# The first loads of a fused attention and feed-forward kernel: another order on the two queues, no touch load, and other fillers on TensorE

## The chip, the cores and the metric

The kernel runs on one core of one Trainium2 chip. The metric is the device time in microseconds (us) of one execution.

## The reference, cut to what matters

```python
x = A_x                                        # 2048 x 640, bf16
g = sigmoid((x * gate_w).sum(-1))
qkv = x @ wqkv                                 # 640 -> 3 * 640
pq, pk = phi(q), phi(k)                        # phi(t) = where(t > 0, t + 1, exp(t)) + 1e-6
a = linear_attention(pq, pk, v) @ wo
b = (gelu(x @ w_gate) * (x @ w_up)) @ w_down   # the larger part
return g * a + (1 - g) * b
```

The change touches only the first 9 us or so: the loading of x and of the K and Q columns of `wqkv`, and the first two of the sixteen 128-row tiles of x, which TensorE transposes itself. All other tiles are transposed by DMA while they are loaded.

## The kernel before

The kernel is a list of operations for each engine. A helper, `P.op`, works out the waits from what each operation reads and writes. `"sp"` is SyncE's DMA queue, `"act"` is ScalarE's. Chunk k of `wk` holds rows 128k to 128k+127 of the K columns; a load of one chunk, or of one tile of x, is 160 KB.

```python
P.op("act", lambda e: e.dma_start(touch[0:16, 0:4], A_wqkv[0:128:8, 640:644]),
     writes=[P.res("touch")], dma=new_dma_key())          # the "touch": 0.1 KB, never read
load_x(0)
load_wk(0)
load_x(1, "act")
load_wk(1)
load_wk(3)
# ... ScalarE's first activation, which loads its table
load_wk(2, "act")
load_wk(4, "act")
# ... gate_w on "act"
for k in range(KC):                                       # KC = 5
    load_wq(k, ("sp", "act")[k % 2])
# ... then on "sp": the transposing loads of x tiles 2 to 15, the first one after wk chunk 4 has landed
```

On TensorE, `warm(count, n)` issues fillers: matmuls of constants with n columns, whose result nobody reads. `T(i, ks, bank)` transposes chunks `ks` of x tile i into a bank of PSUM (the memory that TensorE writes to), and VectorE copies them from there into `xT`. `KM(i, [k])` is the pair of matmuls (512 and 128 columns) of tile i with wk chunk k. `QM` is the same for Q.

```python
def T(i, ks, tb):
    # ... transposes into psb[:, tb, ...]
    P.op("pe", fn, reads=[r_xn[i], r_ident], writes=[bank[tb]])
    P.op("dve", lambda e: e.tensor_copy(xT[:, ks[0]:ks[-1] + 1, i * 128:(i + 1) * 128], ...),
         reads=[bank[tb]], writes=[...])

warm(5, 512)
warm(1, 128)
T(0, [0], 7)
T(0, [1, 2, 3, 4], 6)
warm(6, 128)
KM(0, [0])
T(1, [0], 7)
T(1, [1, 2, 3, 4], 6)
warm(3, 128)
KM(1, [0])
for k in (1, 2, 3):
    KM(0, [k])
    KM(1, [k])
gate_col()
# ... KM(0, [4]), KM(1, [4]), then QM for both tiles, all five chunks
```

## Time and profile before

| | before |
|---|---|
| median of 3 executions | 274.09 us (273.87 to 274.1) |
| span of the profiled execution | 272.2 us (its device time: 273.55 us) |
| x tile 0 landed / wk chunk 0 landed | 3.0 / 4.24 us |
| first K matmul / first Q matmul | 4.38 / 7.67 us |

The page of the kernel before gives the span, and then each engine's busy time with its share of the span. PE is TensorE, PEld its weight loads, DVE VectorE, ACT ScalarE and POOL GpSimd; below, SPq and ACTq are the queues of SyncE and ScalarE, and PEq is TensorE's sequencer.

```profile
span 272.2 us, 3426 instructions
...
PE 267.9 (98%) x1343; PEld 128.1 (47%) x1369; DVE 141.8 (52%) x251; ACT 75.9 (28%) x132; POOL 30.0 (11%) x28
```

TensorE is busy for 98% of the span, so only its head can give anything. Below is TensorE's timeline of the kernel before. The columns are start, duration (both in us), engine, line, operation with its operands, and count; at the end stands the idle time before it, with what ended that. Consecutive instructions of one kind are merged.

```profile
0.82 2.40 PE L417 MATMUL ps<-const-bfloat16-1.0 128*128 128x512 bf16 x6 [0.82 <-PEq L911]
3.02 0.74 PE L431 MATMUL ps<-pool 128*128 128x128 bf16 x5
3.55 0.62 PE L417 MATMUL ps<-const-bfloat16-1.0 128*128 128x128 bf16 x6
4.38 0.38 PE L451 MATMUL ps<-pool 128*128 128x512 bf16 x1 [0.21 <-DMA pool<-in_A_wqkv_dram]
...
4.64 0.44 PE L431 MATMUL ps<-pool 128*128 128x128 bf16 x5
...
5.18 0.39 PE L451 MATMUL ps<-pool 128*128 128x512 bf16 x1
...
6.01 0.38 PE L451 MATMUL ps<-pool 128*128 128x512 bf16 x1
...
7.67 0.38 PE L466 MATMUL ps<-pool 128*128 128x512 bf16 x1
7.88 0.22 PE L467 MATMUL ps<-pool 128*128 128x129 bf16 x1
```

L417 is the fillers, L431 the transposes, L451 and L452 a K pair, L466 and L467 a Q pair. The first six fillers (five of 512 columns, one of 128) run from 0.82 to 3.02 us. That is 0.43 us for each wide one, twice what a wide matmul takes later: the K pairs that follow each other at 0.27 us contain one wide matmul (0.22 us) and one narrow one. TensorE's clock is still low there. The six narrow fillers at 3.55 us are the place where it rises.

Next come two of the waits of TensorE and of its weight loads in the first 12 us. The columns are who waited for what, us in total, times, and the longest.

```profile
PE ps L451 <- DMA pool<-in_A_wqkv_dram: 0.2, 1, 0.2
```

```profile
PEld ps L451 <- DVE pool L435: 0.4, 1, 0.4
```

The first K pair waited 0.2 us for wk chunk 0; the weight load of tile 1's first K pair waited for VectorE's copy. The next lines are from the chain of work that ended last, in order of time (start, us, what):

```profile
1.26 2.98 DMA pool<-in_A_wqkv_dram
...
4.38 0.38 PE ps L451
...
10.32 0.71 ACT pool L476
...
16.89 9.15 PE ps L536 x49
```

The chain starts with the load of wk chunk 0 (issued at 1.26 us). It goes through the K and Q matmuls, then through ScalarE and VectorE until 16.9 us, and from there through TensorE to the end. So whatever moves the first Q matmul should move the end by as much. Last, the first two DMA issues (size, us from issue to landing):

```profile
pool<-in_A_x_dram SPq DMA_DIRECT2D x1, 160.0 KB, 2.2
pool<-in_A_wqkv_dram ACTq DMA_DIRECT2D x1, 0.1 KB, 2.0
```

x tile 0, issued at 0.79 us, landed 2.2 us later. The touch of 0.1 KB took 2.0 us, so the whole of x tile 0 costs only 0.2 us more than a load of almost nothing.

### The profile page before, as it was taken

The numbers are of one execution on the slowest core, as the hardware profiler recorded it, in microseconds if no ns is written. First come the engines' busy times: TensorE is split into PE (matmuls) and PEld (weight loads), VectorE is DVE, ScalarE is ACT, GpSimd is POOL, SyncE is SP. The second block draws the span as 40 slices with busy tenths as digits, with TensorE's granted clock in tenths as the row PEclk, the third lists the DMA queues.
The fourth block names the chain that finished last, engine by engine and source line by source line (L and its number), as shares of the span: only waits on it lengthen the run. The fifth ranks groups of instructions, "written<-read, shape, count | busy, mean of one in ns | idle before, by whom it ended". The sixth has DMA issues, their size and how long they took to land.

```text
span 272.2 us, 3426 instructions
## 1 busy us (share of the span) xinstructions
PE 267.9 (98%) x1343; PEld 128.1 (47%) x1369; DVE 141.8 (52%) x251; ACT 75.9 (28%) x132; POOL 30.0 (11%) x28
## 2 busy tenths in 40 slices
PE   8999999999999999999999999999999999999997
PEld 4555555544445444444444444444444444444444
DVE  2689898997333335999999999634110000000200
ACT  2555555210422453332222232224011122121021
POOL 5000000003140002242332421000000000000000
PEclk9999999999999999999999999999999999999999
DMA  6776999500300011612221221272031110110211
GB/s 219 176 114 124 349 402 384 119 2 19 61 16 2 23 50 51 200 28 48 27 48 30 43 50 25 60 229 96 5 79 37 41 39 19 39 41 19 58 58 41
DMA packets 42208, 23.61 MB, mean 87 GB/s; under 512 B 31567, under 2 KB 40783, under 8 KB 42063
## 3 DMA queue, kind: packets, MB, share of 16 engines
q1 hardware_dynamic: 41429, 22.56, 30.5%
q10 hardware_dynamic: 762, 0.82, 0.8%
q8 instruction: 11, 0.18, 0.3%
q14 instruction: 6, 0.05, 0.1%
HBM read 13.83 MB, written 2.63 MB: 60 GB/s over the span
## 4 chain that ended last, share of the span: by engine, by line
PE 95%; DVE 2%; DMA 1%; issue 1%; ACT 1%; SPq 0%; DVEq 0%; ACTq 0%
PE ps L697 41%; PE ps L861 23%; PE ps L536 12%; PE ps L593 6%; PE ps L840 4%; PE ps L808 2%; PE ps L675 2%; PE ps L596 2%; DMA pool<-in_A_wqkv_dram 1%; PE ps L451 1%; PE ps L821 1%; PE ps L466 1%; DVE pool L490 1%; PE ps L718 1%; DVE pool L555 1%
## 5 line engine op out<-in xcount | busy, mean ns | idle before, releaser
L697 PE MATMUL ps<-pool 128*128 128x512 bf16 x510 | 113.0, 379 | 0.5
L697 PEld LDWEIGHTS ps<-pool 128*128 128x128 bf16 x520 | 50.4, 98 | 60.1
L861 PE MATMUL ps<-pool 128*128 128x512 bf16 (+2 forms) x300 | 62.4, 367 | 0.3
L703 ACT ACTIVATE pool<-ps 128x512 f32<-128x512 f32 x52 | 31.0, 597 | 73.1 <-PE ps L697 73.1
L705 DVE TENSOR_TENSOR pool<-ps,pool 128x512 bf16<-128x512 f32 x52 | 34.6, 689 | 31.7 <-PE ps L697 30.4
L861 PEld LDWEIGHTS ps<-pool 128*128 128x128 bf16 x306 | 29.1, 98 | 33.5 <-issue 0.4
L536 PE MATMUL ps<-pool 128*128 128x512 bf16 (+1 forms) x206 | 37.9, 344 | 0.2
L844 DVE TENSOR_TENSOR pool<-ps,pool 128x512 bf16<-128x512 f32 x4 | 2.8, 692 | 61.5 <-PE ps L840 61.5
L751 POOL TENSOR_TENSOR pool<-pool 128x640 f32<-128x640 bf16 x16 | 22.5, 1406 | 72.8 <-DVE pool L753 65.9
L868 ACT ACTIVATE pool<-ps,pool 128x512 bf16<-128x512 f32 (+1 forms) x16 | 10.9, 680 | 68.6 <-PE ps L861 68.6
L536 PEld LDWEIGHTS ps<-pool 128*128 128x128 bf16 x210 | 20.5, 98 | 17.5
L555 DVE SCALAR_TENSOR_TENSOR pool<-ps,pool 128x128 bf16<-128x128 f32 (+2 forms) x42 | 25.3, 603 | 2.4
L546 ACT ACTIVATE pool<-ps 128x640 bf16<-128x640 f32 x28 | 19.7, 703 | 18.1 <-DVE pool L555 10.6
L593 PE MATMUL ps<-pool 128*128 128x512 bf16 x76 | 19.2, 380 | 0.1
L761 DVE TENSOR_TENSOR pool<-pool 128x640 bf16<-128x640 bf16 x16 | 13.2, 825 | 0.6
L759 DVE TENSOR_SCALAR pool<-pool 128x32 f32<-128x32 f32 x16 | 12.8, 803 | 0.6
L753 DVE TENSOR_REDUCE pool<-pool 128x32 f32<-128x640 f32 x16 | 12.9, 809 | 0.0
L641 DVE TENSOR_TENSOR pool<-pool 128x640 f32<-128x640 f32 x14 | 11.6, 826 | 0.5
L840 PE MATMUL ps<-pool 128*128 128x512 bf16 x51 | 11.5, 380 | 0.1
L643 POOL PARTITION_ALL_REDUCE pool<-pool x1 | 4.0, 3971 | 60.7 <-DVE pool L641 60.7
L593 PEld LDWEIGHTS ps<-pool 128*128 128x128 bf16 x78 | 6.9, 98 | 7.2
L552 DVE TENSOR_SCALAR pool<-pool 128x640 bf16<-128x640 bf16 x28 | 9.1, 327 | 1.8 <-ACT pool L546 0.4
(70 smaller groups left out, 105.0 us busy)
## 6 DMA issues: line engine op xcount, KB each, us to landing
out_dram<-pool SPq DMA_DIRECT2D x19, 128.0 KB, 1.7
pool<-in_B_w_gate_dram SPq DMA_DIRECT2D x1, 2080.0 KB, 14.2
pool<-in_B_w_up_dram SPq DMA_DIRECT2D x1, 2080.0 KB, 18.8
pool<-in_A_x_dram SPq DMA_DIRECT2D x1, 1280.0 KB, 8.7
pool<-in_B_w_down_dram SPq DMA_DIRECT2D x1, 1120.0 KB, 6.1
pool<-omg_row SPq DMA_DIRECT2D x1, 1024.0 KB, 4.8
pool<-in_A_wqkv_dram SPq DMA_DIRECT2D x6, 160.0 KB, 4.4
pool<-in_A_x_dram SPq DMA_DIRECT2D x1, 960.0 KB, 5.8
```

The source lines that it names most:

```text
L536: last = e.matmul(ps[:, b + p, 0:c1 - c0], xT[:, k, i * 128:(i + 1) * 128], wkq[:, k, c0:c1], start=(k == 0), stop=(k == KC - 1))
L546: P.op("act", lambda e: e.activation(e_buf[m], ps_flat[:, o:o + 640], ACT.Exp), reads=banks, writes=[r_e[m]])
L555: P.op("dve", lambda e, c0=c0, c1=c1: e.scalar_tensor_tensor(dst[:, c0:c1], ps_flat[:, o + c0:o + c1], 1.0 + EPS, e_buf[m][:, c0:c1], ALU. ...
L593: last = e.matmul(ps[:, b, :], pk[i][:, c * 128:(c + 1) * 128], x_aug[:, i, 0:512], start=(i == 0), stop=(i == NT - 1))
L697: last = e.matmul(ps[:, b, :], w[:, k, fc * 128:(fc + 1) * 128], xT[:, k, j * 512:(j + 1) * 512], start=(k == 0), stop=(k == KC - 1))
L703: P.op("act", lambda e: e.activation(ge[n], ps[:, gb, :], ACT.Gelu_apprx_tanh), reads=[bank[gb]], writes=[r_ge[n]])
L705: P.op("dve", lambda e: e.tensor_tensor(hT[fc][:, j * 512:(j + 1) * 512], ps[:, ub, :], ge[n], ALU.mult), reads=[bank[ub], r_ge[n]], write ...
L751: P.op("pool", lambda e: e.tensor_tensor(tmp[n], pq[i], z_b, ALU.mult), reads=[r_pq[i], r_zb], writes=[r_tmp[n]])
L753: P.op("dve", lambda e: e.tensor_reduce(den[n], tmp[n].rearrange("p (h d) -> p h d", h=32), AX.X, ALU.add), reads=[r_tmp[n]], writes=[r_de ...
L761: P.op("dve", lambda e: e.tensor_tensor(pq[i].rearrange("p (h d) -> p h d", h=32), pq[i].rearrange("p (h d) -> p h d", h=32), den[n].unsqu ...
L840: last = e.matmul(ps[:, b, :], wd[:, fc, 512:640], hT[fc][:, j * 512:(j + 1) * 512], start=False, stop=(fc == NFC - 2), skip_group_check=True)
L861: last = e.matmul(ps[:, pb, 0:c1 - c0], lhs, rhs, start=False, stop=(q == len(rows) - 1), skip_group_check=True)
```

## The change

The intent is to have x tile 0 and wk chunk 0 arrive together at the heads of both queues, then tile 1 and chunk 1. The touch load goes. TensorE gets two more wide fillers, so that it stays busy until x tile 0, now sharing the bandwidth, lands. Tile 0's second K pair is drawn forward, and three fillers stand in front of the pairs of chunk 2.

```diff
--- before.py
+++ after.py
@@ -352,22 +352,20 @@
                 dma_in(wq[:, k, 0:640], A_wqkv[k * 128:(k + 1) * 128, 0:640], [r_wq[k]], eng=eng)
 
 
-            P.op("act", lambda e: e.dma_start(touch[0:16, 0:4], A_wqkv[0:128:8, 640:644]),
-                 writes=[P.res("touch")], dma=new_dma_key())
             load_x(0)
-            load_wk(0)
-            load_x(1, "act")
-            load_wk(1)
-            load_wk(3)
+            load_wk(0, "act")
+            load_x(1)
+            load_wk(1, "act")
+            load_wk(2)
+            load_wk(4)
 
             zero = nc.const_aps.tensor(0.0, (128, 1), F32)
             P.op("act", lambda e: e.activation(eg[:, 0:1], zero, ACT.Exp), writes=[r_eg[0]])
-            load_wk(2, "act")
-            load_wk(4, "act")
+            load_wk(3, "act")
             P.op("dve", lambda e: e.memset(gw_sb, 0.0), writes=[r_gw])
             dma_in(gw_sb[0:5, :], gate_w.rearrange("(k p) -> k p", p=128), [r_gw], eng="act")
             for k in range(KC):
-                load_wq(k, ("sp", "act")[k % 2])
+                load_wq(k, ("act", "sp")[k % 2])
 
             def load_xT(i, after=()):
                 P.op("sp", lambda e: e.dma_start_transpose(xT[:, :, i * 128:(i + 1) * 128],
@@ -500,17 +498,19 @@
 
 
             ALLK = list(range(KC))
-            warm(5, 512)
-            warm(1, 128)
+            warm(7, 512)
+            warm(2, 128)
             T(0, [0], 7)
             T(0, [1, 2, 3, 4], 6)
-            warm(6, 128)
+            warm(3, 128)
             KM(0, [0])
             T(1, [0], 7)
             T(1, [1, 2, 3, 4], 6)
+            KM(0, [1])
+            KM(1, [0])
+            KM(1, [1])
             warm(3, 128)
-            KM(1, [0])
-            for k in (1, 2, 3):
+            for k in (2, 3):
                 KM(0, [k])
                 KM(1, [k])
             gate_col()
```

## The prediction

> **What bounds it now.** TensorE is busy in 98% of the 272.2 us span (engine table), so only the head can give anything. TensorE's timeline: fillers from 0.82 us; transposes of x tile 0 at 3.02; first K matmul at 4.38, after a 0.21 us wait for wk chunk 0; transposes of x tile 1 at 4.64; then K pairs every 0.27 us; first Q matmul at 7.67. From there the chain of waits runs through the Q matmuls, ScalarE and VectorE (10.3 to 16.9 us), then TensorE to the end: a shift of the first Q matmul should pass on one for one.
>
> **Loads before** (landing, DMA view): x0 3.0, wk0 4.24, x1 4.4, wk1 5.4, wk2 5.6, wk3 6.2, wk4 6.5, wq0 7.4 us: 160 KB at 3.0, then 320 KB per 1.0 to 1.3 us. The Trainium skill ("DMA: Bandwidth & Descriptors", "Issuing engines are not separate DMA queues") says that issuing from two engines only saves issue time; the trace agrees: pairs share about 300 GB/s.
>
> **After, costed.**
> - x0 shares the head with wk0 in place of a 0.1 KB touch. Estimate: both land near 3.5 (half a pair after the old x0). wk0 gains 0.7 us, x0 loses 0.5.
> - Seven fillers of 512 columns. Until about 3.7 us the trace shows them 0.43 us apart (half rate; 128-column ones then go from 107 to 56 ns). The Trainium skill ("TensorE: Matmul & The Clock Gate", "What's actually happening") has TensorE start at half rate until a busy window of about 3.4 us has passed; here that ends near 3.7. So the fillers end near 3.85 and themselves hold x0's transposes, 0.8 us later than before, though at full rate.
> - From a transpose group's start to its first K matmul: 0.54 us (tile 1: 4.64, copy 4.90, matmul 5.18). So KM(0,0) starts near 4.40, against 4.38: the wait for wk0 goes, VectorE's copy behind a late transpose stands in its place.
> - x1 and wk1 land near 4.8 (4.5 to 5.0): x1 later than its 4.4, wk1 earlier than 5.4. T(1) starts near 4.8 instead of 4.64.
> - KM(1,1) needs tile 1's second copy (copies last 0.65 us from 0.26 after the transposes' start): about 5.8 (before 5.74). Three fillers (0.17 us) now follow: KM(0,2) near 6.2 (before 6.01). wk2, wk3 (5.9) and wk4 (6.6) are in time; six pairs and the gate column take 1.65 us: first Q matmul at 7.75 to 7.95, against 7.67.
> - wq chunks land within 0.2 us of before, with 0.3 us or more of slack: hidden.
>
> All of the change lies on the critical path, but its parts cancel: -0.2 us (wk0), +0.2 to +0.4 (late transposes, x1 later, fillers before k=2). After the first Q matmul the instructions are the same.
>
> **Predicted: 274.2 us, 8 in 10 between 273.7 and 274.7. Faster by over 2%: 0.005; within 2%: 0.985; slower: 0.01.**
>
> **What would show the steps.** x0 and wk0 landing near 3.5; T(0) near 3.85 right behind a filler; no wait for wk0; T(1) starting on x1's landing; KM(1,1) released by VectorE's copy; first Q matmul 0.1 to 0.3 us later; the 10.3 to 16.9 us stretch shifted by as much.
>
> **What would make it wrong.** Two queues fill faster at the start (gain up to 0.2 us); x0 landing past 3.9; the clock rising at another moment, which moves the fillers' end by up to 0.4 us; a wq chunk or the first transposing load of x becoming late.

## More of the kernel before

The trace's record of the granted clock has its first entry, full clock, at 3.77 us. **The profile's own row of granted clocks does not show this.** Here are two windows of the kernel before; the columns are the window, its length, the busy time and count of each engine, then the granted clock, the DMA share and GB/s:

```profile
0.00:2.00 2.00, 1.18 (x3) 0.43 (x4) 0.11 (x1) 0.29 (x1) 1.12 (x7) 1.00 0.07 19
2.00:4.00 2.00, 2.00 (x15) 1.27 (x13) 0.43 (x2) 1.20 (x2) 1.86 (x3) 1.00 0.89 253
```

Both say 1.00, although the first two microseconds ran at half rate: nothing is recorded before the rise. At the head of a kernel the clock has to be read from the durations.

## The result, and the profile after

| | before | after |
|---|---|---|
| median | 274.10 us (4 executions, 273.87 to 274.29) | 274.33 us (4 executions, 273.76 to 274.76) |
| ratio after / before | | 1.0008, 95% interval 0.9986 to 1.0029 |
| the same in two more sessions | | 1.0006 (0.9993 to 1.0019) and 1.0017 (1.0005 to 1.0029) |

A ratio is the mean time of one kernel's fast runs over that of the other's fast runs of the same rounds, so it is not quite the ratio of the medians. The three sessions put the change at 0.2 to 0.5 us slower, though only the third interval excludes no change at all: "the same" at the 2% level, and close to the predicted 274.2 us.

The execution that was profiled after the change was the slowest of its four (274.76 us), whereas the one profiled before (273.55 us) was faster than the four other executions of it in this comparison. The two traces therefore exaggerate the difference.

TensorE's timeline after (L415 fillers, L429 transposes, L449 and L450 K pairs, L464 and L465 Q pairs):

```profile
0.83 3.36 PE L415 MATMUL ps<-const-bfloat16-1.0 128*128 128x512 bf16 x9 [0.83 <-PEq L911]
4.03 0.56 PE L429 MATMUL ps<-pool 128*128 128x128 bf16 x5
...
4.64 0.39 PE L449 MATMUL ps<-pool 128*128 128x512 bf16 x1
...
4.92 0.59 PE L429 MATMUL ps<-pool 128*128 128x128 bf16 x5
...
6.03 0.39 PE L449 MATMUL ps<-pool 128*128 128x512 bf16 x1
...
6.31 0.34 PE L415 MATMUL ps<-const-bfloat16-1.0 128*128 128x128 bf16 x3
7.30 0.39 PE L449 MATMUL ps<-pool 128*128 128x512 bf16 x1 [0.66 <-DMA pool<-in_A_wqkv_dram]
...
8.97 0.38 PE L464 MATMUL ps<-pool 128*128 128x512 bf16 x1
9.19 0.22 PE L465 MATMUL ps<-pool 128*128 128x129 bf16 x1
```

The transposes of tile 0 start at 4.03 us, 1.0 us later than before. The first K pair at 4.64 us is only 0.26 us later, and it no longer waits for a load. The pairs of chunk 2 come at 7.30 us instead of 6.01, after a wait of 0.66 us; the first Q matmul comes at 8.97 us instead of 7.67. The waits view (0 to 12 us) says the same, and shows a wait for VectorE, which copies tile 1:

```profile
PE ps L449 <- DMA pool<-in_A_wqkv_dram: 0.7, 1, 0.7
```

```profile
PEld ps L449 <- DVE pool L433: 0.3, 1, 0.3
```

The DMA issues after: first the two at the heads of the queues, then wk chunk 2 (issued at 1.72 us).

```profile
pool<-in_A_wqkv_dram ACTq DMA_DIRECT2D x1, 160.0 KB, 3.0
pool<-in_A_x_dram SPq DMA_DIRECT2D x1, 160.0 KB, 3.2
```

```profile
pool<-in_A_wqkv_dram SPq DMA_DIRECT2D x1, 160.0 KB, 5.5
```

Issued at 0.78 and 0.79 us, wk chunk 0 landed at 3.80 us and x tile 0 at 3.99. The intent was met: they arrive together, TensorE is busy until then, and the wait for wk chunk 0 is gone. But x tile 0 pays with 1.0 us. wk chunk 2 took 5.5 us. The trace counts the landing of a load in sixteen parts: fourteen of chunk 2's had arrived by 6.03 us, the last two at 6.47 and 7.26. The last share cost this execution the 0.66 us. It was not late alone: in the next three loads on SyncE's queue, too, the last share came 0.75 to 1.2 us after the fifteenth.

### The profile page after: what moved, and what is told of

The parts are those of the page before. It is cut to its first block, busy times and chain, and to the rows that moved or that the text cites. A ratio compares the mean times of both kernels' runs of the same rounds, so it can differ in the third digit from the quotient of the medians.

```text
span 273.5 us, 3425 instructions
## 1 busy us (share of the span) xinstructions
PE 268.8 (98%) x1343; PEld 128.3 (47%) x1369; DVE 141.8 (52%) x251; ACT 75.9 (28%) x132; POOL 30.0 (11%) x28
## 4 chain that ended last, share of the span: by engine, by line
PE 94%; DMA 2%; DVE 2%; issue 1%; ACT 1%; SPq 0%; DVEq 0%; ACTq 0%
PE ps L697 41%; PE ps L861 23%; PE ps L536 11%; PE ps L593 6%; PE ps L840 4%; DMA pool<-in_A_wqkv_dram 2%; PE ps L808 2%; PE ps L675 2%; PE ps L596 2%; PE ps L821 1%; PE ps L464 1%; DVE pool L488 1%; PE ps L449 1%; PE ps L718 1%; DVE pool L555 1%
```

## The experiments

Twelve kernels were run, each with 5 rounds beside the kernel before on the same chip. There were three sessions: runs e1 to e4, e5 to e8, and e9 to e12. In the sessions the kernel before had medians of 273.88, 273.99 and 274.12 us. All runs gave correct results.

**One relation ties them together.** In each of the fourteen traces, the device time of the profiled execution less the start of the second matmul of the first Q pair (L467 in the kernel before) is between 265.5 and 265.7 us. This matmul starts at 7.88 us in the fastest of the traces and at 11.15 us in the slowest. So, in these traces, everything that happens to the time happens before the first Q pair. The time of an execution without a trace then gives an estimate of when its Q pairs began: 273.98 us, the mean of all 42 executions of the kernel before, means 8.4 us, and not the 7.88 us of the profiled one. (The second matmul is used because one trace lacks the record of the first.)

### e1: the changed kernel again

No edit.

> The changed kernel unchanged, for a second trace. Theory A (the steps of the prediction: late transposes, x tile 1 later, fillers before the k=2 pairs, together +0.1 to +0.3 us; the further 0.8 us of the first profile is one DMA engine that finished its share of wk chunk 2 late by chance): first Q matmul at 7.8 to 8.1 in this trace, wk chunk 2 landed before 6.3, ratio 1.000 to 1.001, single times spread over up to 1 us. Rival B (the order of the loads makes wk chunk 2 late every time): wk chunk 2 lands after 6.8 again, first Q matmul past 8.6, ratio about 1.003.

Measured: 274.14 us median (273.98 to 274.29), ratio 1.0006 (0.9993 to 1.0019). wk chunk 2 landed at 6.21 us, the first Q matmul started at 8.26 us. The late chunk 2 of the first trace is therefore not a fixed result of the order. The chain of work of this run:

```profile
0.82 3.36 PE ps L415 x9
4.18 0.53 PE ps L429 x5
4.72 0.25 PE ps L415 x3
4.96 0.21 PE ps L449
...
5.24 0.40 PE ps L429 x5
...
6.18 0.37 PE ps L449
...
6.60 0.17 PE ps L415 x3
```

This is the chain that the prediction drew: nine fillers, the transposes, three fillers, K pairs, the transposes of tile 1, a K matmul that had to wait for VectorE's second copy (its piece is 0.37 us long because it does not overlap the matmul before it; it is no slower), and three more fillers. No load is on it, not even x tile 1, for which the prediction had the second transposes wait.

### e2: the new loads with the old TensorE program

```diff
 # after's loads; TensorE as before:
-warm(7, 512); warm(2, 128) ...
+warm(5, 512); warm(1, 128); T(0...); warm(6, 128); KM(0, [0]); T(1...); warm(3, 128); KM(1, [0]); for k in (1, 2, 3): ...
```

> The new loads with the old TensorE program (fillers 5+1, then 6, then 3; both tiles' k=0 first). Theory A: five fillers end near 3.0, x tile 0 lands at 3.5 to 4.0, so its transposes now wait for the DMA by 0.5 to 1.0 us instead of following a filler; first K matmul at 4.2 to 4.6, first Q matmul 7.7 to 8.0, ratio 1.000 to 1.001. If instead the seven fillers are what costs, this is 0.2 to 0.4 us faster than the whole change, and faster than before.

Measured: 275.82 us median (274.37 to 276.53), ratio 1.0070 (1.0051 to 1.0090). This is far more than expected, and the trace happened to catch the fastest execution. TensorE's timeline there:

```profile
3.77 0.72 PE L429 MATMUL ps<-pool 128*128 128x128 bf16 x5 [0.55 <-DMA pool<-in_A_x_dram]
```

The fillers end at about 3.0 us, and TensorE idles until x tile 0 lands, 0.55 us by the profile. By the relation above, the mean execution (275.65 us) had its Q pairs begin at about 10.0 us. This led to a theory for the following runs, called D there: the work lost in the gap puts off the rise of the clock, in most executions.

### e3: the old loads with the new TensorE program

Edit: the kernel before, with the changed `warm`, `T` and `KM` sequence.

> The old loads with the new TensorE program. Theory A: the seven fillers hold x tile 0's transposes until about 3.9 to 4.1 although the tile landed at 3.0; the second K pair of tile 0 waits for wk chunk 1, which lands at 5.4 in this order; first Q matmul at 8.0 to 8.3, so 0.3 to 0.6 us slower than before (ratio 1.001 to 1.002). If the fillers' order cost nothing: ratio 1.000.

Measured: 274.62 us median (273.93 to 274.66), ratio 1.0016 (1.0001 to 1.0031), 0.5 us in the means, as expected. x tile 0 landed at 3.05 us, but its transposes stood behind the fillers until 3.98 us. The rest of the way was not the expected one. wk chunk 1 landed at 5.18 us, and the second K pair of tile 0 did not wait for it: that pair started at 5.90 us, still at half rate, because the clock rose only between 5.90 and 6.30 us, with no gap in TensorE's work before it. The first Q matmul came at 8.73 us, later than the expected 8.0 to 8.3. Each half of the change alone is slower than before. But e3 cannot be told from the whole change (1.0006 in e1, 1.0017 in e12): the intervals overlap.

### e4: the change, with the touch load put back

```diff
+P.op("act", lambda e: e.dma_start(touch[0:16, 0:4], A_wqkv[0:128:8, 640:644]), ...)
 load_x(0)
 load_wk(0, "act")
```

> The changed kernel with the touch load put back at the head of the ScalarE queue. Theory A: it only delays the ScalarE queue's loads by one issue (0.45 us): wk chunk 0 lands 0.2 to 0.4 us later and x tile 0 somewhat earlier; ratio to before within 0.001 of the whole change's. Rival C (the touch wakes the queue, and its removal is what makes the first loads slow: x tile 0 at 3.99 instead of the estimated 3.5): x tile 0 lands by 3.4 and the time falls by 0.3 us or more.

Measured: 274.63 us median (274.2 to 275.77), ratio 1.0028 (1.0011 to 1.0046). The expectation of a ratio within 0.001 of the whole change's was missed (1.0028 against 1.0006, though the intervals overlap). x tile 0 landed at 3.13 us, as rival C had it, but the time did not fall, so C as it was stated falls as well. The touch takes the first place on ScalarE's queue: x tile 0 has the bandwidth to itself, while wk chunk 0 (4.56 us) and chunk 1 (6.13 us, with a late last share, for which TensorE waited 0.59 us) come later. That it is a matter of sharing can be seen in the DMA packets. Here are those from 1.5 to 2.7 us, first of the kernel before, then of the changed one (q1 is SyncE's queue, q10 ScalarE's; the columns are packets, MB, and share of the 16 engines):

```profile
q1 hardware_dynamic: 171, 0.20, 65.3%
q10 hardware_dynamic: 32, 0.00, 1.4%
```

```profile
q10 hardware_dynamic: 72, 0.09, 38.4%
q1 hardware_dynamic: 34, 0.04, 13.2%
```

In both traces the first packets start at 1.8 us. With the touch nearly all the bytes are SyncE's, which begin with x tile 0; without it x tile 0 and wk chunk 0 move side by side. The two together moved less than SyncE's queue alone did before (0.14 MB in the unrounded sum, against 0.20), so whether the touch also helps the start in another way stays open. The trace of e4 also names a wait that the prediction had overlooked, in its waits of the weight loads (0 to 12 us):

```profile
PEld ps L431 <- DVE pool L435: 0.2, 1, 0.2
```

Tile 1's last four transposes (L431 in this kernel) wait for VectorE (L435) to copy tile 0's out of the same PSUM bank. Before, the order gave VectorE more time.

### e5: the kernel before, again

> The kernel before, unchanged, against itself: the noise. Ratio within 0.001 of 1, single times 273.5 to 274.7. Theory D (the spread of single times is the moment at which TensorE's clock rises, which differs from run to run: 3.8, 4.3, 4.8, 5.7 and 5.9 us in the traces so far): this trace's clock may rise at another moment than 3.77 us, and the first Q matmul then moves from 7.67 by about half of the time between 4.4 us and the rise. If the rise is always 3.8 in this kernel, its phase is not left to chance.

Measured: 273.75 us median (273.45 to 274.13), ratio 0.9995 (0.9982 to 1.0007). The clock rose at 4.03 us, the first Q matmul started at 7.75 us. This is the noise: 0.0005 in the ratio, and 1.2 us between the extremes of all executions of the kernel before (273.45 to 274.68).

### e6: e2 with the long fillers

```diff
 # e2, and:
-warm(5, 512); warm(1, 128)
+warm(7, 512); warm(2, 128)
```

> The run with the new loads and the old TensorE order, which was 0.7% slower than before, with one thing put in: the seven plus two fillers of the change in place of five plus one. Theory D (a gap in TensorE's work while x tile 0 is on its way delays the clock's rise[...] in most executions): the time falls by 1 to 2 us to 274.1 to 274.5, ratio 1.000 to 1.002. Rival E (the order of the K pairs is what cost): it stays at 275.5 or more.

Measured: 274.62 us median (273.97 to 274.94), ratio 1.0025 (1.0011 to 1.0039). Three fillers took e2's ratio from 1.0070 to 1.0025, about 1.2 us (0.0045 of 274 us), although they add work to TensorE. The two ran on different chips, each beside the kernel before, and the intervals do not overlap. So it was not chiefly the order of the K pairs (rival E), and the long fillers pay for themselves with the new loads. The result stayed just above the expected range.

### e7: the kernel before with short fillers

```diff
-warm(5, 512)
+warm(1, 512)
 warm(1, 128)
```

> The kernel before with one filler of 512 columns in place of five; loads and everything else as before, so TensorE sits idle from about 1.4 to 3.0 us. Theory D: the clock rises later (5 to 8 us), K pairs run at half rate until then, and the time grows by 0.5 to 2.5 us (ratio 1.002 to 1.009). Rival: the fillers do nothing for the clock, and the time stays within 0.3 us of before, because x tile 0 is awaited until 3.0 us anyhow.

Measured: 275.19 us median (274.54 to 276.82), ratio 1.0047 (1.0030 to 1.0064). The profiled execution is the slowest, and TensorE's timeline shows why:

```profile
3.06 0.71 PE L431 MATMUL ps<-pool 128*128 128x128 bf16 x5 [1.55 <-DMA pool<-in_A_x_dram]
...
5.20 0.59 PE L451 MATMUL ps<-pool 128*128 128x512 bf16 x1 [0.78 <-DMA pool<-in_A_wqkv_dram]
...
6.54 0.63 PE L451 MATMUL ps<-pool 128*128 128x512 bf16 x1
...
7.07 0.63 PE L451 MATMUL ps<-pool 128*128 128x512 bf16 x1
...
10.66 0.38 PE L451 MATMUL ps<-pool 128*128 128x512 bf16 x1
```

There are gaps of 1.55 and 0.78 us, and the wide K matmuls are 0.63 us long (0.38 us at full clock) until the clock rises; the trace's record of the clock puts that at 10.47 us. A K pair takes 0.53 us (6.54 to 7.07) instead of 0.27. The program's loads are the same as before, but in this execution the last share of wk chunk 0 was late (5.06 us, the fifteenth at 4.44), which made most of the second gap: the slowest execution is not all the fillers' doing. In the mean the missing fillers cost 1.3 us (0.0047 of 274 us), although x tile 0 was awaited until 3.0 us in both programs. What the fillers buy is the clock, not the covering of a wait.

### e8: the kernel before without the touch

Edit: the touch load deleted, nothing else.

> The kernel before without the touch load and nothing else, one part of the change alone. x tile 0 now shares the head of the queues with x tile 1 and lands at 3.5 to 3.7 instead of 3.0; the five fillers end at 3.0, so there is a gap of 0.5 to 0.7 us before its transposes. Theory D: like the run with the new loads alone, 1 to 2 us slower in most executions (ratio 1.003 to 1.008). If a gap of that size does no harm: at most 0.3 us slower (ratio up to 1.001).

Measured: 274.20 us median (273.65 to 275.5), ratio 1.0020 (1.0000 to 1.0039), less than expected. x tile 0 landed at 3.91 us instead of 2.97, beside x tile 1 instead of beside the touch. In the trace TensorE idled 0.73 us before the transposes, and K pairs ran at half rate until about 7.1 us. But other executions (273.65, 274.02 us) were as fast as before. If their gaps were as long (they were not traced), a gap of that size does not always put off the clock. Why e2, whose traced execution had a shorter gap, lost more than this is open.

### e9: the kernel before with its own gap filled

```diff
-warm(6, 128)
+warm(9, 128)
 KM(0, [0])
```

> The kernel before with nine instead of six 128-column fillers after x tile 0's transposes, so that TensorE stays busy until wk chunk 0 lands at 4.2 to 4.3 (today there is a gap of 0.2 us, or none where the clock is still low). Theory D: the clock rises no later than before, in executions where that gap matters sooner; the fillers delay the first K matmul by at most 0.2 us. Ratio 0.998 to 1.001. If it is faster by 0.3 us, the gap matters and this version beats both.

Measured: 274.23 us median (273.79 to 274.66), ratio 1.0004 (0.9991 to 1.0017). No gain is seen (a gain of 0.3 us would lie just outside the interval). In this trace, with the gap filled, the clock rose at 4.32 us, against 3.77 and 4.03 us in the two traces of the kernel before. One trace says little, but it does not bear out that the rise comes no later.

### e10: the change without the late fillers

```diff
 KM(1, [1])
-warm(3, 128)
 for k in (2, 3):
```

> The changed kernel without the three fillers between the k=1 and the k=2 pairs. By the prediction's sum they cost 0.17 us: first K pair of chunk 2 right behind the last pair of chunk 1 where chunk 2 has landed, first Q matmul 0.17 us sooner, ratio to before lower by 0.0006 than the whole change's. Rival: chunk 2 lands after them anyhow (7.26, 6.21 in the two traces against 6.5), so they are free and the time stays.

Measured: 274.02 us median (273.63 to 274.49), ratio 0.9999 (0.9986 to 1.0012), against 1.0017 for the whole change in the same session. In the trace the first pair of chunk 2 follows the last pair of chunk 1 directly (6.52 us; chunk 2 had landed at 6.30). In e1 and e12 the three fillers stand in front of that pair although its chunk had landed, so they are not free there: the traces put them at 0.17 us, the prediction's figure. The means are 0.5 us apart, but the intervals overlap, and how much of that the fillers make stays uncertain.

### e11: the change with fewer fillers at the head

```diff
-warm(7, 512)
-warm(2, 128)
+warm(6, 512)
+warm(1, 128)
```

> The changed kernel with six plus one fillers in place of seven plus two, which end at 3.45 instead of 3.98. If the fillers are what holds x tile 0's transposes (the prediction's step), those start on its landing at 3.5 to 3.8, 0.2 to 0.5 us sooner, and so does all that follows, ratio 0.999 to 1.000. Theory D: where the gap that opens is over 0.2 us, the clock rises[...] later in some executions, and the mean gets worse, as with five fillers (1.007): ratio 1.001 to 1.005.

Measured: 274.19 us median (273.89 to 274.7), ratio 1.0003 (0.9991 to 1.0015). It sits between the two expectations: better than theory D feared, worse than the gain that the earlier transposes promised. The trace (TensorE's timeline) shows both the earlier start, behind a short wait for x tile 0, and where it went:

```profile
3.83 0.45 PE L429 MATMUL ps<-pool 128*128 128x128 bf16 x5 [0.18 <-DMA pool<-in_A_x_dram]
...
7.74 0.39 PE L449 MATMUL ps<-pool 128*128 128x512 bf16 x1 [0.30 <-DMA pool<-in_A_wqkv_dram]
```

The transposes began 0.15 us sooner and the clock rose at 3.85 us, so that the first K pair started at 4.38 us. Then the last share of wk chunk 4 was late (7.69 us, the fifteenth at 6.22), and the pair at 7.74 us waited 0.30 us for it. In every wq load after it the last share came 1.3 to 1.7 us after the fifteenth.

### e12: the changed kernel, a third time

No edit.

> The changed kernel once more, beside the three others and for a third trace. Ratio 1.0000 to 1.0020; first Q matmul at the run's time less 265.8 us to within 0.1 us, as in the ten traces so far; wk chunk 2 landing anywhere from 5.9 to 7.3 if one late DMA engine is chance.

Measured: 274.58 us median (274.42 to 274.81), ratio 1.0017 (1.0005 to 1.0029). wk chunk 2 landed at 5.45 us, even earlier than expected, so the late share of the first trace is not fixed by the order of the loads. (Single late shares appear with both orders: wk chunk 0 at 5.06 us in e7, which has the old loads.) The first Q matmul started at 8.69 us all the same. TensorE's timeline shows the cause:

```profile
3.98 0.74 PE L429 MATMUL ps<-pool 128*128 128x128 bf16 x5
...
4.83 0.63 PE L449 MATMUL ps<-pool 128*128 128x512 bf16 x1
...
5.37 0.69 PE L429 MATMUL ps<-pool 128*128 128x128 bf16 x5
5.90 0.38 PE L449 MATMUL ps<-pool 128*128 128x512 bf16 x1
```

The first wide K matmul took 0.63 us, and the transposes of tile 1 follow each other into 5.90 us at 0.11 us each. The clock rose only shortly before 5.90 us, with TensorE busy from 0.83 us without a gap that the profile shows. (The moment comes from the durations: the traces of e2, e3, e8 and e12 hold no record of the rise at all.)

## Why the prediction was right or wrong

The predicted time (274.2 us, 273.7 to 274.7) held: 274.33 us, and 274.14 and 274.58 us in the repeats. The net effect was forecast as +0.1 us and measured as +0.2 to +0.5 us. The hit itself proves little: the range is 1.0 us wide, about as wide as the spread of single executions, and would have held if the change had done nothing. Point by point:

- **A shift of the first Q matmul passes on one for one: right.** This held in all fourteen traces to within 0.1 us or so.
- **x tile 0 and wk chunk 0 near 3.5 us, close to each other: right in kind, too early by up to 0.5 us.** The three traces have 3.99 and 3.80, 3.70 and 3.50, 3.85 and 4.04 us. x tile 0 loses 0.7 to 1.0 us instead of 0.5.
- **The fillers hold the transposes until 3.85 us: right, slightly mis-sized.** Seven fillers at 0.43 us and two at 0.107 us end at 3.98 us, because the clock rose after that time in all three traces. In the first trace x tile 0 came later still, by 0.05 us.
- **The first K pair at 4.40 us: this term was mis-sized.** The prediction carried the rise of the clock (3.7 us) over from its one trace. It took the 0.54 us from the start of the transposes to the first K matmul from tile 1 of the kernel before, which ran at full clock. Measured are 0.61, 0.82 and 0.85 us, because the clock rose at 4.29, 4.75 and shortly before 5.90 us. The first K pair came at 4.64, 4.80 and 4.83 us, so the gain of 0.2 us for wk chunk 0 never reached it: the parts did not cancel as the prediction said. In e1, which no late load disturbs, the first Q matmul is 0.60 us later than before: 0.43 us of it is there at the first K pair, and 0.17 us comes after.
- **T(1) starts when x tile 1 lands: wrong.** Tile 1 had landed (4.78, 4.48, 4.66 us). T(1) followed the first K pair directly. Inside T(1) came the unforeseen wait for the PSUM bank that e4 names.
- **KM(1,1) released by VectorE's copy, then 0.17 us of fillers: right.** It is on e1's chain, and e10 without these fillers was faster in its session, though the intervals overlap.
- **The first Q matmul at 7.75 to 7.95 us: wrong in these traces** (8.97, 8.26, 8.69 us). The forecast of the total held nevertheless, because the baseline of 7.67 us was too low as well: the profiled execution before was a fast one. By the relation between time and Q start, the mean before is at 8.4 us and the mean after, from its 14 timed executions (274.35 us), at 8.75 us, both for the pair's second matmul.
- **"The clock rising at another moment" was listed as a danger of 0.4 us. It was a larger one.** The three traces of the changed kernel have rises from 4.29 to about 5.9 us, and between e1 and e12 the later rise makes the difference of 0.43 us in the first Q matmul.

Left open: the clock of e2's slow executions was not traced (that it rose late there is argued from e6 and e7, not shown); why a gap hurts in e2 and e7 and less in e8 (a late rise in one trace is no proof of a gap's effect, since e3 and e12 rose late without one; the effect rests on the means of e2 against e6, and of e7); and what makes the last share of a load late. No version beats the kernel before beyond noise: the best, e10, stands at 0.9999.

How the Trainium skill was used. "TensorE: Matmul & The Clock Gate", section "What's actually happening", states a half clock at the start, a busy window of about 3.4 us before the full clock, and a window that runs freely. The half rate agrees with the fillers' 0.43 us against 0.22 us, and the moving moment of the rise agrees too; the length of the window is not measured by any run here. "DMA: Bandwidth & Descriptors", section "Issuing engines are not separate DMA queues", says that loads from several engines interleave on the same DMA engines. The trace agrees: beside another 160 KB load on the other queue, x tile 0 landed at 3.7 to 4.2 us (eight traces) instead of 3.0 to 3.1 (six traces with the touch).

## What to carry to other kernels

Putting two loads at the heads of two queues does not speed up both: here they shared the bandwidth, so decide which one the first useful instruction needs. While TensorE's clock is still low, fillers that close a gap can be worth more than the time they take, and a duration measured at full clock must not be used in a sum for the first few microseconds. For changes of a few tenths of a microsecond one trace on each side misleads; find the instruction from which on everything is the same, and use the time of many executions to place it.

## What the Trainium skill lacked or had wrong

- "TensorE: Matmul & The Clock Gate", section "What you observe", puts the rise at about 4 us of sustained work, give or take 0.5 us. Here, counted from the first filler at 0.82 us, it came after 2.95 us (the kernel before), after 5.1 us in e12 and after 5.1 to 5.5 us in e3, both without a gap. In e7 TensorE worked without a gap from 5.20 us, and the rise came 5.3 us later. The page calls the number of slow matmuls variable from run to run; the spread here is wider than its 0.5 us.
- No page says that a profile's row of granted clocks reads 1.00 before the first recorded change (windows 0 to 2 and 2 to 4 us of the kernel before, while wide fillers took 0.43 us instead of 0.22), or that the rise can be missing from the record (four of fourteen traces). The nearest is a warning in "TensorE: Matmul & The Clock Gate", section "Seeing it yourself", that recorded clock events have been seen to be unreliable.
- "DMA: Bandwidth & Descriptors", section "Latency and other measured facts", speaks of two DMA engines that are usually slower, and ties it to software-made descriptors. Here all loads are issued by hardware queues, and still the last share of a 160 KB load came 0.8 us after the fifteenth of sixteen (6.47 and 7.26 us, wk chunk 2 in the first trace after) and up to 1.7 us (a wq chunk in e11), in some executions and not in others, and then in load after load. Which engine it was, the trace does not tell.
